# A hand-ordered attention and long-convolution kernel: paired VectorE products and a new order of work

## The chip, the cores and the metric

The kernel runs on one NeuronCore of a Trainium2 chip. It uses five engines, each with its own in-order stream of instructions: TensorE (PE) for matmuls and transposes, VectorE (DVE) and ScalarE (ACT) for elementwise work, GpSimd (POOL) and SyncE (SP), which here mostly issue DMAs. Engines wait for each other by semaphores. The metric is the device time of one execution in microseconds (us); lower is better.

## The reference

Two blocks follow each other. The first is attention with 4 batches, 8 heads, 768 positions and head size 64. A query sees the first 8 keys (global) and the 96 keys up to itself (local); each head has its own slope for a bias that falls with distance. The second is a gated long convolution over the 512 channels.

```
scores = scale * q @ k.T + bias           # bias = -slope[h] * distance
scores = where(is_global | is_local, scores, -1e9)
a = softmax(scores);  x = a @ v           # x: [4, 768, 512]

x1, x2, x3 = split(x @ w_proj, 3)         # 512 columns each
x2_conv = irfft(rfft(x2) * rfft(filter))  # over the 768 positions
out = (x1 * x2_conv * x3) @ w_out
```

All inputs and the output are float32. The kernel computes in float16 with float32 accumulation.

## The kernel before, in words

**Tiling.** Work is done batch by batch, with up to two batches in flight: while `conv(b)` runs, `attention(b + 1)` is mixed into it. Within attention, heads go in four pairs (`hp` 0 to 3) and the keys in seven tiles of 128 (8 global keys and 120 local ones each), which form three groups (`GRP`, group index `gi`, tiles 0-1, 2-3 and 4-6). Of the 768 by 768 scores only a band is computed.

**Attention.** `load_pair` loads q or k of a pair, `turned` transposes it on TensorE and copies it to `QT` or `KT`. For batch 3, `load_tiles` loads q and k by tiles and `cross` transposes them with DMA transposes from SP. `scores` multiplies a pair and group into two PSUM banks, and one ScalarE exponential (line 774) reads both banks and writes 864 elements per partition of the pair's tile `E`. For batch 0 ("near") the bias and mask are added to the scores on TensorE. For batches 1 to 3 the exponential is multiplied by a table of masks on VectorE (line 791). The branch at line 779 can do this for two pairs at once, but `PAIR_M`, the list of the batches and groups that take it, is empty. `values` multiplies `E` by v, `rc` and `xn` divide by the sum, and `transpose_x` turns the result into `xT`.

**Gates and convolution.** `gate` computes x1 and x3 from `xT` and the weights `w`, four matmuls each (line 932). `butterfly` and `conv` do the Fourier transform of x2 as small matmuls and VectorE additions ("proj", line 993; "fwd", lines 676, 690 and 1124; "inv", lines 1023 to 1030). In `spectra` each pair of class spectra X is multiplied on VectorE by two filter tables, `h1` and `h2` (lines 1142 and 1145), into `p1` and `p2`, which are halves of one tile `pp`. Another `conv` step multiplies by the gates and projects with `wo` (line 1059); the result `ot` is stored by SP (line 1070).

**The start.** k0, q0 (pair 0 of batch 0) and k1 come as three 384-KB loads from SP and are cast to float16 ("cast", line 314). The other pairs of batch 0, the filter (768 KB), v, the weights `w` (four loads of 256 KB and one of 512 KB), `wo` and everything of the later batches come from POOL (`load`, line 339), in loads of mostly 96 to 120 KB. The identity used by the transposes is made on POOL between the first loads, and so are the tables of distances. ScalarE makes the sine tables of the transform first, then switches its function table to the exponential. Dummy matmuls ("busy", line 310) stand early in TensorE's stream.

**What sets the order.** `Plan` records about a thousand operations with their dependencies. Nothing schedules them at run time: the string `ORDER` at the top of the file lists every operation by its number, with the engine that does it (P, A, V, G, S) and the PSUM banks it takes, and `schedule` only checks that dependencies precede. `i1b5` puts one dummy matmul on bank 5. So the order of each engine, the choice between ScalarE and VectorE for an evacuation, the sequence of the loads on POOL and that of SP's queue all come from this one text. The waits themselves come from the data.

The functions that the change touches:

Of the kernel before, what the change touches and what calls it, by code (L numbers as in the profile page):

```python
# [17 lines left out]
P = 128  # L18
# [14 lines left out]
def dve(n, rate=1, psum=False):  # L33
    return 0.068 + (0.005 if psum else 0.0) + n / rate / 960.0
# [8 lines left out]
35G 19A 12P2 13A 46V 52G 37A 48V i2b5 83P0 38A 53G 81P3 72G 20V 26A 61G 63G 21A 14V 44V 50V 15V 39V 201P1 93P2  # L43
36V 87P4 84A 202V 57V 60G 43A 82A 207V 95P3 16A 94A 97P67 209V 85P2 65G 64G 29V 11V 62G 88A 41V 91P0 203V 66G
96V 149P45 239G 42A 236G 86V 98A 204A 234G 150A 40V 89P3 121P67 151P45 238G 58V 208V 90V 205V 122A 152A 117P23
92V 99P67 206V 103P45 211V 233G 212V 118A 213V 235G 100A 119P23 101P67 153P01 104A 105P45 120A 102A 154A 27V
214V 115P23 237G 106V 215V 59S 116A 107V 155P67 78A 216V 110P01 111V 128P23 232G 157P45 156A 77A 217V 67G
220P6 112V 162P01 221A 158V 108P6 73A 113P7 129V 130V 123P23 109A 224P6 159V 131P4 114V 79A 222P7 245G 68G
341P5 241G 243G 225A 163V 124V 76A 223A 218P6 31V 240G 164V 125V 337P0 132V 28V 339P1 244G 340V 165P7 126P4
127V 247G 160P2 74A 335P1 338A 137P4 342A 166V 193V 139A 161V 133P7 376P23 219A 242G 336V 246G 354P45 414P01  # L50
377A 138P6 69G 167P2 355A 134P3 415A 183V 135A 184V 351P45 352A 192V 194V 140V 373P01 186V 185V 136V 343P6
374A 459G 169A 248G 195V 172P7 70G 71G 171P4 464G 187V 196V 173A 226P01 347P2 227A 345P3 411P45 251G 344V 252G
353V 349P0 145P6 75A 174V 249S 412A 348V 141P2 346V 254G 357P45 350V 228A 417P01 147A 375V 253G 420P67 188V
168P3 255G 197V 458G 256G 470G 356V 189V 143A 170V 142P2 465G 418A 471G 144V 175P0 358A 146P1 421A 382P67 198V
191V 460G 360P23 177A 413V 199V 148V 80A 190V 383A 379P45 380A 258P0 463G 361A 259A 229P67 416V 200V 378V
271P1 363P45 272A 230A 422V 275P2 461G 364V 273P3 231A 250S 466G 276A 284P6 419V 385P01 362V 274A 384V 286P7
359V 260P2 386V 365V 387V 462G 560P3 287A 479G 478G 285A 469G 261A 368P45 381V 279P0 366P1 472G 561A 473G 369V
468G 277P2 288V 423P67 370V 280A 262P3 289V 264P0 278A 367A 371P1 424V 263A 467G 425V 372A 282V 566P2 428P45
266P1 390P67 257G 265A 706G 567A 562P0 281V 267A 429V 388P3 391V 563A 179P2 430V 564P1 392V 176P4 181A 180P0
565A 389A 269V 576P67 268V 182V 178V 426P1 577A 431P2 393P0 432V 427A 394V 579P45 687G 580A 598P67 639P23 640A  # L60
396P0 698G 572P1 574P4 270V 395P5 298P2 407P3 696G 573A 599A 474G 397A 450V 570P1 568P6 449V 451V 695G 452V
404P5 575A 299A 408P7 694G 409A 403P4 571V 684G 398V 636P23 585P01 453V 410V 690G 569A 283V 454V 405A 600V
637A 582P67 445P4 480G 586A 481G 699S 399P2 447A 406V 433P3 446P4 455V 477G 702G 292P5 583A 435A 401A 456V
457V 645P67 607P01 448V 693G 293A 300P3 638V 646A 290P2 294P5 441P4 295A 304P6 442P5 581V 476S 608A 482G 584V
443A 400P7 475S 578V 302P4 697G 296P0 609V 688G 301A 291A 647V 303A 444V 689G 402V 485P1 604P45 297A 305A 587V
642P23 486A 307V 306V 605A 601P67 641V 691G 643A 685S 483P0 496P1 593P23 602A 308V 594V 603V 497A 484A 498P4
606V 588P67 487P5 589V 683G 701G 499A 595A 437P4 309V 489P0 590V 490A 488A 704G 310V 615P67 439A 692G 644V
311V 703G 610P23 611V 616V 700S 653P01 491P5 617A 438P4 612V 312V 511P2 440V 654V 686S 434P3 313V 596P4 618P6
512A 597A 492A 619A 500P7 655V 591P2 592A 613P5 314V 493V 501A 502P4 509P6 494V 648P01 504P7 656P2 705G 614A
624P5 510A 787S 649V 505A 513V 657A 632P6 503A 436V 315V 620P7 507V 629P4 621P3 626A 323P5 495V 506V 789S 514V  # L70
625P2 650A 508V 785S 634A 622A 651P0 324A 652A 628P6 784S 515P7 786S 517P5 529P1 518A 623V 527P3 627V 316V
675V 523P0 516A 528A 519P2 630A 670P5 525P3 793S 526A 521P7 633P6 530A 520A 791S 332P3 674V 317P2 524A 635V
333A 631V 672A 662P3 522A 803P45 790S 677V 806P67 800P01 318A 664A 801A 788S 676V 326P2 804A 795S 532V 327A
329P3 320P0 678V 330A 321A 796S 707P2 679V 663P3 807A 797P01 531V 680V 794S 825P67 533V 708A 534V 822P45 798A
682V 826A 720P2 666P0 535V 805V 536V 665V 671P3 823A 537V 681V 828P67 673V 721A 819P45 711P1 658P3 668A 820A
712A 799V 792S 829A 724P2 861P01 827V 870P67 660A 867P45 725A 722P3 540V 538V 802V 319S 334S 871A 733P2 868A
539V 723A 709P6 809P45 726P3 541V 734A 808V 554P7 331S 872V 810V 727A 735P3 542P2 830V 811V 862A 863V 555A
710A 814P01 836P45 864P67 736A 815V 543A 824V 837V 667P3 816V 865A 659P2 869V 838A 866V 715P6 713P7 661V
878P01 325S 669V 714A 548P2 728P7 812P3 879V 716A 821V 880V 737V 817P6 831P45 729A 873P01 839P7 322S 832V 730V
818A 813A 874V 551P3 731V 833A 875V 328S 732V 718V 557P6 881P4 738V 834P5 876P0 545P1 840A 835A 882A 877A  # L80
856P7 556S 717V 841P4 904V 741P0 903V 719V 745P5 546A 749P1 558A 742A 843A 549A 746A 857P6 842P0 906V 905V
907V 908V 851P2 858A 909V 750A 753P7 559S 844A 747P5 754A 739P4 743P1 751P0 883P7 744A 912P1 748A 910V 740A
852P4 752A 756V 859A 755V 913A 924P6 853A 936P2 552A 925A 911V 884P5 757V 854A 938P6 914P3 845V 937A 758V
916P2 939A 915A 860V 928P3 759V 888P6 210A 917A 760V 553S 940V 761V 929A 920P4 550S 918P3 886A 919A 926P2 941V
764V 921A 923V 922V 932P3 889P5 927A 898P4 933A 930P3 544S 894P2 885A 946P7 931A 762V 896A 942P3 935V 957P1
846P2 934V 855V 947A 958A 961P7 943A 944P1 962A 948P3 945A 763V 959P0 949A 963P7 960A 964A 765V 951V 950V
847P1 781P0 547S 891A 965V 966V 952V 967V 769P5 899P7 848A 953V 770A 900A 968V 954V 969V 772P2 955V 970V 956V
766P3 849A 773A 971V 850V 974V 774S 901A 972V 893P2 767A 782A 975V 775P7 973V 890A 892V 778P3 771S 895A 897V
982P2 768S 985V 779A 902V 783S 976P3 887V 776A 979P7 986V 983A 987V 993P2 989P6 988V 780S 994P 1001P0 980V
990P 777S 977A 978S 997P7 998P 995A 984S 991A 999A 1002P 1003V 981S 996S 992S 1000S 1004S  # L90
"""


# [105 lines left out]
class Fused:  # L199
# [541 lines left out]
    def scores(self, hp, gi, near=False):  # L741
        nc, g = self.nc, self.g
# [23 lines left out]
        if self.b in self.CROSS:  # L766
# [3 lines left out]
                                    name="near" if near else "scores"))  # L770
# [8 lines left out]
        if (self.b, gi) in self.PAIR_M:  # L779
            if hp % 2:  # L780
                hs = slice(2 * hp - 2, 2 * hp + 2)
                ep = self.EE[:, hp - 1:hp + 1].rearrange("p a h c -> p (a h) c")[
                    :, :, 496 * gi:496 * gi + 496].rearrange("p h (m w) -> p h m w", m=2)[:, :, :, 0:216]
                mk = self.mask[:, hs].rearrange("p h (m w) -> p h m w", m=3)
                mk = (mk[:, :, 0:2], mk[:, :, 1:2].to_broadcast([P, 4, 2, 216]), mk[:, :, 1:3])[gi]
                g.op("V", dve(1728, 2), lambda _: nc.vector.tensor_mul(ep, ep, mk),
                     r=[("mask", h) for h in range(hs.start, hs.stop)], w=[("E", hp - 1, gi), ("E", hp, gi)], name="masked")
            return
        mk = self.mask[:, 2 * hp:2 * hp + 2].rearrange("p h (m w) -> p h m w", m=3)
        mk = (mk[:, :, 0:2], mk[:, :, 1:2].to_broadcast([P, 2, 2, 216]), mk[:, :, 1:3])[gi]  # L790
# [1 line left out]
             r=[("mask", 2 * hp), ("mask", 2 * hp + 1)], w=[("E", hp, gi)], name="masked")  # L792
# [324 lines left out]
    def spectra(self, b, pair):  # L1117
        nc, g, X, DM = self.nc, self.g, self.X, self.DM
# [11 lines left out]
        if n == 2:  # L1130
# [11 lines left out]
        g.op("V", dve(1024, 2), lambda _: nc.vector.tensor_mul(  # L1142
            p1, xs, self.h1[:, n:n + 1].to_broadcast([P, 2, DM])),
             r=rs, w=[("p1", k)], name="prod")
        g.op("V", dve(1024, 2), lambda _: nc.vector.tensor_mul(
            p2, xs, self.h2[:, n:n + 1].to_broadcast([P, 2, DM])),
             r=rs, w=[("p2", k)], name="prod")

        if b in self.SUMPE:
            return  # L1150
# [147 lines left out]
```

## Time and profile before

| What | Value |
| --- | --- |
| median of 3 runs | 164.43 us (164.33 to 164.94) |
| profiled execution | 164.8 us |
| its span, first to last instruction | 163.0 us |
| granted TensorE clock | 0.999 |
| PE busy | 154.0 us (94%) |
| VectorE busy | 151.6 us (93%) |
| ScalarE busy | 150.3 us (92%) |
| POOL busy | 76.8 us (47%) |
| bytes moved by DMA | 21.95 MB |

The profile is of one execution. "Span" runs from the first to the last instruction; the execution's own time is 1.8 us longer. A busy share counts the time in which at least one instruction of the engine was in flight; neighbouring instructions overlap, so the distance between two starts is often shorter than a duration. A row of a timeline or of the chain gives the start in us, the length in us, the engine, the line of the code, and what it writes and reads; "x4" says that four instructions were merged. "[1.85 <-ACT y L498]" says that the engine stood idle for 1.85 us before it, until ScalarE's instruction of line 498 was done.

### The profile page before, as it was taken

The numbers are of one execution on the slowest core, as the hardware profiler recorded it, in microseconds if no ns is written. First come the engines' busy times: TensorE is split into PE (matmuls) and PEld (weight loads), VectorE is DVE, ScalarE is ACT, GpSimd is POOL, SyncE is SP. The second block draws the span as 40 slices with busy tenths as digits, with TensorE's granted clock in tenths as the row PEclk, the third lists the DMA queues.
The fourth block names the chain that finished last, engine by engine and source line by source line (L and its number), as shares of the span: only waits on it lengthen the run. The fifth ranks groups of instructions, "written<-read, shape, count | busy, mean of one in ns | idle before, by whom it ended". The sixth has DMA issues, their size and how long they took to land.

```text
span 163.0 us, 4256 instructions
## 1 busy us (share of the span) xinstructions
PE 154.0 (94%) x1604; PEld 94.7 (58%) x1604; DVE 151.6 (93%) x356; ACT 150.3 (92%) x327; POOL 76.8 (47%) x101
## 2 busy tenths in 40 slices
PE   6599997999999999999999999999999999999980
PEld 2274355866655777666577584445676664584440
DVE  6599699999999999999999999999999999999960
ACT  8999996999999999999999999999998999997850
POOL 7999199999979997999970000000000000000000
PEclk9999999999999999999999999999999999999999
DMA  5999999999999999999999964630100106000684
GB/s 170 200 166 164 165 150 138 147 158 174 190 162 154 139 136 136 149 153 163 161 129 162 134 121 101 236 150 0 64 4 6 66 0 253 5 4 0 264 332 178
DMA packets 84956, 21.95 MB, mean 135 GB/s; under 512 B 75584, under 2 KB 81992, under 8 KB 84936
## 3 DMA queue, kind: packets, MB, share of 16 engines
q0 software_dynamic: 73040, 12.11, 98.4%
q1 hardware_dynamic: 11896, 9.57, 21.4%
q8 instruction: 12, 0.20, 0.5%
q14 instruction: 8, 0.07, 0.1%
HBM read 25.40 MB, written 6.29 MB: 194 GB/s over the span
## 4 chain that ended last, share of the span: by engine, by line
PE 85%; ACT 9%; DVE 3%; issue 1%
PE bank L932 26%; PE bank L993 13%; PE bank L1059 13%; PE bank L759 7%; PE bank L854 4%; PE bank L809 4%; PE bank L707 3%; PE bank L1023 3%; PE bank L1124 3%; PE bank L814 3%; PE bank L753 2%; ACT E L774 2%; ACT KT L314 1%; PE bank L1030 1%; PE bank L690 1%; ACT QT L314 1%
## 5 line engine op out<-in xcount | busy, mean ns | idle before, releaser
L932 PE MATMUL bank<-xT,w 128*128 128x384 f16 x256 | 48.2, 326 | 0.0
L774 ACT ACTIVATE E<-bank 128x864 f16<-128x864 f32 x48 | 41.0, 911 | 0.3 <-PE bank L759 0.2
L932 PEld LDWEIGHTS <-w 128*128 128x128 f16 x256 | 23.9, 98 | 15.8 <-issue 0.3
L339 POOL DMA_DIRECT2D vn<-in_v_dram x28 | 26.3, 979 | 1.1 <-DMA w<-in_moe_w_proj_dram 1.1
L339 POOL DMA_DIRECT2D kn<-in_k_dram x25 | 21.8, 892 | 5.4 <-DMA vn<-in_v_dram 4.0
L1059 PE MATMUL bank<-wo,y 128*128 128x512 f16 (+1 forms) x100 | 22.6, 371 | 0.0
L339 POOL DMA_DIRECT2D qn<-in_q_dram x25 | 21.8, 885 | 0.1
L791 DVE TENSOR_TENSOR E<-E,mask 128x864 f16<-128x864 f16 x36 | 20.3, 591 | 0.0
L318 ACT ACTIVATE x<-bank 128x384 f16<-128x384 f32 x32 | 16.6, 547 | 0.0
L318 ACT ACTIVATE ot<-bank 128x512 f32<-128x512 f32 (+1 forms) x23 | 13.3, 610 | 3.5 <-PE bank L1059 3.1
L809 PE MATMUL bank<-vn,E 128*128 128x65 f16 x224 | 15.3, 193 | 0.9 <-DVE xn L833 0.7
L993 PE MATMUL bank<-w,xs 128*128 128x512 f16 x64 | 15.9, 379 | 0.0
L809 PEld LDWEIGHTS <-E 128*128 128x128 f16 x224 | 14.0, 97 | 2.3 <-DMA vn<-in_v_dram 0.4
L1059 PEld LDWEIGHTS <-y 128*128 128x128 f16 x100 | 9.5, 98 | 9.9 <-DVE y L1113 0.5
L814 PE MATMUL bank<-vn,E 128*128 128x65 f16 x192 | 15.0, 193 | 0.0
L314 ACT CAST eo<-bank 128x384 f16<-128x384 f32 x32 | 14.3, 513 | 0.6 <-PE bank L1030 0.2
L314 ACT CAST X<-bank 128x512 f16<-128x512 f32 x24 | 14.3, 636 | 0.4
L314 ACT CAST ab<-bank 128x512 f16<-128x512 f32 x24 | 14.3, 629 | 0.4 <-PE bank L993 0.3
L833 DVE TENSOR_TENSOR xn<-bank,rc 128x512 f16<-128x512 f32 (+1 forms) x19 | 14.3, 771 | 0.1
L814 PEld LDWEIGHTS <-E 128*128 128x128 f16 x192 | 13.1, 97 | 1.9 <-issue 1.2
L759 PE MATMUL bank<-QT,KT 64*128 64x216 f16 (+2 forms) x224 | 13.7, 242 | 0.0
L759 PEld LDWEIGHTS <-KT 64*128 64x128 f16 x224 | 7.9, 94 | 8.7 <-issue 6.8
(163 smaller groups left out, 334.1 us busy)
## 6 DMA issues: line engine op xcount, KB each, us to landing
out_dram<-ot SPq DMA_DIRECT2D x23, 256.0 KB
vn<-in_v_dram POOLq DMA_DIRECT2D x28, 120.0 KB, 7.6
kn<-in_k_dram POOLq DMA_DIRECT2D x16, 96.0 KB, 5.1
qn<-in_q_dram POOLq DMA_DIRECT2D x16, 96.0 KB, 5.2
w<-in_moe_w_proj_dram POOLq DMA_DIRECT2D x4, 256.0 KB, 5.8
kn<-in_k_dram POOLq DMA_DIRECT2D x7, 120.0 KB, 6.2
g<-in_moe_filter_fft_dram POOLq DMA_DIRECT2D x1, 768.0 KB, 10.6
qn<-in_q_dram POOLq DMA_DIRECT2D x6, 128.0 KB, 7.0
```

The source lines that it names most:

```text
L314: {"A": nc.scalar.copy, "V": nc.vector.tensor_copy, "G": nc.gpsimd.tensor_copy}[e](out, in_)
L318: self.nc.scalar.mul(out, in_, c)
L339: return self.g.op(eng, 0.57 + 0.00035 * nbytes[0] if eng == "G" else 0.5, lambda _: e.dma_start(dst, src), w=w, r=r, nbytes=nbytes, name= ...
L759: nc.tensor.matmul(bs[hh].f32()[:, off:off + w], self.KT[hs, hp, P * m:P * m + P], self.QT[hs, hp, KL * m:KL * m + w], start=(off == 0 and ...
L774: g.op("A", act(864), lambda _: nc.scalar.activation(eo, bs[0].two()[:, :, 0:432].rearrange("p h (m w) -> p h m w", m=2), Act.Exp, scale=s ...
L791: g.op("V", dve(864, 2), lambda _: nc.vector.tensor_mul(eo, eo, mk), r=[("mask", 2 * hp), ("mask", 2 * hp + 1)], w=[("E", hp, gi)], name=" ...
L809: nc.tensor.matmul(o[:, n, hh], ef[:, at:at + P], vt[:, t, 2 * hp + hh, 0:D + 1], start=first, stop=(t == 0), skip_group_check=True)
L814: nc.tensor.matmul(o[:, n, hh], ef[:, at:at + P], vt[:, t - 1, 2 * hp + hh, 0:D + 1], start=False, stop=True, skip_group_check=True)
L833: nc.vector.tensor_mul(to, o[:, :, :, 0:D], rc.to_broadcast([P, 2, 2 * nt, D]))
L932: nc.tensor.matmul(bk.f32()[:, 0:h], self.w[:, c, o + P * j:o + P * j + P], self.xT[:, c, h * s:h * s + h], start=(c == 0), stop=(c == 3))
L993: nc.tensor.matmul(bk.f32(), src[:, c], w[:, c, DM:2 * DM], start=(c == 0), stop=(c == 3))
L1059: nc.tensor.matmul(bk.f32()[:, 0:n], y[:, c, P * t:P * t + P], self.wo[:, c, cs], start=(c == 0), stop=(c == 3))
```

## The change

Three edits are made.

1. `PAIR_M` now lists batches 1 to 3 with all three groups. For these, the mask product is done when the second pair of two has its exponential, as one VectorE instruction of 1728 elements per partition instead of two of 864. There are 18 such instructions instead of 36.
2. `h1` and `h2` become halves of one tile, and the two products of a class pair become one instruction that writes `p1` and `p2`, 2048 elements instead of twice 1024. There are 8 instead of 16. The two products of the last class pair of each batch are left as they are.
3. `ORDER` is replaced. Operations keep their code but change places, some evacuations and small copies change between ScalarE and VectorE, the loads on POOL and the DMAs on SP have another sequence, and there are 8 dummy matmuls instead of 3. The loads themselves are the same.

```
-    PAIR_M = ()
+    PAIR_M = tuple((b, gi) for b in range(1, 4) for gi in range(3))
...
-        self.h1 = t("h1", [P, 4, DM])
-        self.h2 = t("h2", [P, 4, DM])
+        self.hh = t("h", [P, 2, 4, DM])
+        self.h1, self.h2 = self.hh[:, 0], self.hh[:, 1]
...
-        pp = t("pp", [P, 2, 4, DM])
+        self.pp = pp = t("pp", [P, 2, 4, DM])
...
-        g.op("V", dve(1024, 2), lambda _: nc.vector.tensor_mul(
-            p1, xs, self.h1[:, n:n + 1].to_broadcast([P, 2, DM])),
-             r=rs, w=[("p1", k)], name="prod")
-        g.op("V", dve(1024, 2), lambda _: nc.vector.tensor_mul(
-            p2, xs, self.h2[:, n:n + 1].to_broadcast([P, 2, DM])),
-             r=rs, w=[("p2", k)], name="prod")
+        g.op("V", dve(2048, 2), lambda _: nc.vector.tensor_mul(
+            self.pp[:, :, 2 * k:2 * k + 2], xs[:, None].to_broadcast([P, 2, 2, DM]),
+            self.hh[:, :, n:n + 1].to_broadcast([P, 2, 2, DM])),
+             r=rs, w=[("p1", k), ("p2", k)], name="prod2")
```

The start of the order, and of the loads in it (operations by kind, in their sequence on the engine):

```
 ORDER, first line
-0V 1V 2A 3G 45S 30A 47S 4V 34V 6A 9A 32G 56S 49S 5V i1b5 22P0 55G 23A 54G 7G 24A 10V 17P1 8V 33V 25V 51G 18A
+0V 1V 2A 3G 4V 5V 45S 32G i1b6 17P0 10V 12P1 8A 33V 22P2 18A 34V 56S 47S 49S 46V 51G 19A 13A 52G 23A 7G 24V
...
 POOL, batch 0 and 1 (b1 q2 is half of pair 2's q of batch 1)
-q3 k3 identity q1 table k2 q2 filter v1 v3 v0 v5 v4 v2 v6 | b1: k1 q1 k0 k1 q0 k0 q1 q0 w0 q3 w1024 q2 k2 q2 q3 k3 k2 k3 w256 | b2 q0, b1 v0, w1280 w512
+q1 k2 identity q2 q3 k3 table filter v0 v6 v1 v2 v5 v3 | b1: k0 k0, v4, w256 k1 k1 q1 q1 w0 q0 q0 w1024 k3 w1280 q3 q3 k2 k2 q2 k3 q2, v0, w512
...
 VectorE, before the first transpose
-... distances, angles 2 (reads ScalarE's result), cast k0, cast q0, angles 1, ..., cast k1
+... distances, cast k0, cast q0, angles 2, angles 1, ...     (cast k1 is on ScalarE)
...
 SP, transposing DMAs of batch 3 among the stores (q1 is q's tile 1)
-q1 q2 q0 k0 k1 q4 q3 k3 k2 q5 k6 k5 k4, then all stores
+q1 q0 q4 q3 q2 k1 q5 k4 k0 k6 k2 k3, two stores, k5, then the other stores
```

More of the change, by code (lines that the diff above doesn't have):

```diff
@@ L47 @@
[L47 to L56, printed above, removed]
@@ new lines @@
+195V 405P01 73A 343P2 180P3 188V 346V 347P6 196V 408A 406A 167P4 181A 253G 344V 189V 348V 450G 341P2 452G 182V
+461G 254G 409V 369P01 376P67 210V 169A 349P45 142P3 370A 171P0 342V 377A 350A 144V 168P1 373V 410P23 255G
+374P45 356P67 197V 173A 270P0 170V 256G 258P1 411A 198V 375A 191V 412P45 200V 190V 199V 378V 271A 357A 353V
+354P23 413A 175P0 355A 272P6 273A 260P4 359P23 358V 259A 262P6 360V 261A 177A 414V 460G 384P45 263A 284P7
+282P1 285A 266P6 264P0 361V 364P23 463G 550P7 385V 283A 276P1 386V 465G 267A 379P45 265A 277A 172P6 365V 286V
@@ L91 @@
+878V 960V 765S 873V 950P3 957A 759S 953P4 961V 951A 958S 952S 967P5 962V 975P3 968P 963P2 976P 964P 954A 977A
+971P4 972P 965A 955S 969V 970S 973V 978S 966S 974S
 """
@@ L786, in scores @@
                 g.op("V", dve(1728, 2), lambda _: nc.vector.tensor_mul(ep, ep, mk),
-                     r=[("mask", h) for h in range(hs.start, hs.stop)], w=[("E", hp - 1, gi), ("E", hp, gi)], name="masked")
+                     r=[("mask", h) for h in range(hs.start, hs.stop)], w=[("E", hp - 1, gi), ("E", hp, gi)], name="masked2")
             return
```

78 lines of the change are left out of this document (40 added, 38 removed).

## The prediction

> **What bounds the kernel now.** I read the page's shares first, then a table by stretches, then the chain of waits in order of time.
>
> ```profile
> PE 154.0 (94%) x1604; PEld 94.7 (58%) x1604; DVE 151.6 (93%) x356; ACT 150.3 (92%) x327; POOL 76.8 (47%) x101
> PE 85%; ACT 9%; DVE 3%; issue 1%
> ```
> ```profile
> 7.16:28.18 21.02, 19.70 (x261) 11.35 (x262) 19.20 (x53) 19.24 (x35) 16.99 (x22) 1.00 1.77 158
> 28.18:60.00 31.82, 31.82 (x391) 21.58 (x388) 31.55 (x80) 31.34 (x61) 30.57 (x37) 1.00 2.04 158
> 60.00:100.00 40.00, 40.00 (x440) 26.49 (x439) 39.80 (x83) 39.76 (x97) 23.25 (x26) 1.00 1.79 143
> 100.00:151.57 51.57, 51.57 (x473) 30.89 (x472) 51.24 (x106) 48.84 (x109) 0.00 (x0) 1.00 0.18 66
> 151.57:163.00 11.43, 6.94 (x37) 3.24 (x34) 5.81 (x17) 4.89 (x10) 0.00 (x0) 0.99 0.73 275
> ```
> ```profile
> 32.97 1.30 PE bank L932 x8
> ...
> 43.08 2.71 PE bank L932 x16
> ...
> 68.80 2.80 PE bank L932 x16
> ...
> 151.57 6.95 PE bank L1059 x36
> 158.55 0.42 DVE ot L320
> ```
> The columns of the second fence are stretch, length, then busy time of PE, weight loads, DVE, ACT and POOL. From 28.2 to 151.6 us TensorE is never idle, VectorE loses 0.8 us and ScalarE 2.8. The chain runs through PE until 158.5. It has small holes all the same: eight matmuls of a gate take 1.30, so sixteen should take 2.60, and the quoted sixteens took 2.71 and 2.80. From such excesses I estimate about 1 us of waiting in the whole stretch. The amount of matmul work isn't changed, so time can come only from an earlier start of the closed run, from those holes, or from the end.
>
> **The change, part by part.**
>
> Merged products. 18 pairs of mask products and 8 pairs of class products become 26 instructions instead of 52.
>
> ```profile
> 49.59 2.10 DVE L791 TENSOR_TENSOR E<-E,mask 128x864 f16<-128x864 f16 x4
> 59.35 0.68 DVE L1145 TENSOR_TENSOR pp<-X,h 128x1024 f16<-128x1024 f16 x1
> 59.95 0.68 DVE L1142 TENSOR_TENSOR pp<-X,h 128x1024 f16<-128x1024 f16 x1
> ```
> Four mask products in a row take 2.10, the last one 0.59 of it, so they start 0.50 apart; two products of a pair start 0.60 apart. 160 more elements for 0.10 us is 0.6 ns each, so 864 elements are about 0.45 to 0.5 and some 0.07 is left per instruction. 26 x 0.07 = 1.8 us off VectorE. The lower end is 0; the upper one takes the whole lag of duration over the elements, 0.68 - 0.53 = 0.15, times 26 = 3.9. I take 1.8, since VectorE runs back to back and what counts there is the distance of starts. [...] None of the 1.8 is on the path by itself, because TensorE is the closed one; it shortens TensorE's waits on VectorE. Of about 1 us of holes I take 0.2 and keep 0 to 1. The price is that the first mask of a pair is ready only after the pair's second exponential; the order places its readers later, so I take nothing for it.
>
> The start. k0, q0 and k1 come by SP; VectorE casts the first.
>
> ```profile
> 2.00:4.00 2.00, 2.00 (x9) 0.89 (x9) 1.49 (x10) 1.94 (x13) 1.71 (x6) 1.00 0.93 320
> ```
> ```profile
> 5.45 0.29 POOL masks.py:199 TENSOR_SCALAR_AFFINE_SELECT ident<-ident 128x128 f16<-128x128 f16 x1
> ```
> ```profile
> 5.89 0.69 DVE L500 SCALAR_TENSOR_TENSOR y<-y,bank 128x512 f32<-128x512 f32 x1 [1.85 <-ACT y L498]
> 6.50 0.61 DVE L314 CAST kn<-h 128x768 f16<-128x768 f32 x1
> ```
> ```profile
> 7.16 0.82 PE L707 MATMUL bank<-ident,kn 128*128 128x128 f16 x6 [1.86 <-DVE kn L314]
> ```
> ```profile
> 8.54 1.07 ACT L314 COPY KT<-bank 128x720 f16<-128x720 f16 x4
> 12.94 1.28 ACT L774 ACT_TABLE_LOAD   x1
> 14.23 0.89 ACT L774 ACTIVATE E<-bank 128x864 f16<-128x864 f32 x1
> ```
> 640 KB had moved by 4 us (320 GB/s), more than k0's 384 KB, yet its cast stood until 6.50 behind an instruction that waited 1.85 for ScalarE. In the new order both casts stand ahead of that instruction, so the transposes of k0 wait for the identity (5.74) instead: 5.8 for 7.16. ScalarE then takes KT at about 6.7 for 8.54. Between KT and the first exponential it does 5.7 us now; there it gains the third cast and two table steps and loses a KT and a QT, about 6.3 in all, so the first exponential comes near 13.0 for 14.2. Five more dummy matmuls of 512 columns stand behind q0, where TensorE has nothing else; at the 0.82 us that 6 x 128 columns take here, each is 0.55. This same ScalarE work hides them; uncovered they would cost 2.7 us. Six other operations move each way between ScalarE and VectorE and nearly cancel; ScalarE's 2.8 idle us cover the rest.
>
> The loads then take most of it back.
>
> ```profile
> 32.90 1.73 POOL L339 DMA_DIRECT2D kn<-in_k_dram  x2
> 34.52 0.86 POOL L339 DMA_DIRECT2D w<-in_moe_w_proj_dram  x1
> ...
> 36.08 1.05 POOL L339 DMA_DIRECT2D vn<-in_v_dram  x1
> 37.01 1.64 POOL L339 DMA_DIRECT2D w<-in_moe_w_proj_dram  x2
> ```
> ```profile
> DMA packets 13844, 2.88 MB, mean 169 GB/s; under 512 B 11596, under 2 KB 13842, under 8 KB 13842
> ```
> ```profile
> kn<-in_k_dram POOLq DMA_DIRECT2D x1, 96.0 KB, 5.2
> w<-in_moe_w_proj_dram POOLq DMA_DIRECT2D x1, 256.0 KB, 5.7
> vn<-in_v_dram POOLq DMA_DIRECT2D x1, 120.0 KB, 5.6
> w<-in_moe_w_proj_dram POOLq DMA_DIRECT2D x1, 256.0 KB, 6.0
> w<-in_moe_w_proj_dram POOLq DMA_DIRECT2D x1, 512.0 KB, 7.9
> ```
> ```profile
> 40.60 0.51 PE L707 MATMUL bank<-ident,kn 128*128 128x128 f16 x6
> ...
> 46.38 1.04 PE L993 MATMUL bank<-w,xo 128*128 128x512 f16 x4
> ```
> The last numbers are us from issue to landing. The last k load of batch 1 is issued at 33.7 and lands at 38.9; the last weights are issued at 37.8 and land at 45.7, and the product that needs them starts at 46.4. So the old order kept 0.7 to 1.7 us of margin. The loads stream without a pause (the DMA column, second to last, stands at 2.04 there) and their bytes don't change; only the sequence does. In the new sequence the last k load of pair 3 has the same loads ahead of it, less one 96-KB load (96 KB at 169 GB/s, 0.6), plus two quarters of the weights. Their cost: 34.5 + 5.7 = 40.2, 1.3 after the k load; 37.0 + 6.0 = 43.0, 1.3 after the v load at 41.7. It lands at 38.9 - 0.6 + 2.6 = 40.9. Its transposes start at 40.6 now, 117.9 before 158.5. By then the new order has done two more gates (2 x 0.65), one pair of transforms (0.43), and one turn (0.34) and two score groups (0.2 each) fewer: 1.0 us more, so 116.9 is left, and PE's work ends at 40.9 + 116.9 = 157.8 instead of 158.5. Everything the start gains beyond that is lost waiting here. Two filter products and the last v loads stand less close. With 0.3 us for an error in six landings I take 0.6 off.
>
> SP. The last transposing DMA, of k tile 5, now stands behind two stores that wait for ScalarE.
>
> ```profile
> 96.95 3.83 SPq L406 DMA_TRANSPOSE KT<-kn  x3
> 101.01 59.10 SPq L1070 DMA_DIRECT2D out_dram<-ot  x25
> ```
> The stores could first be issued at 101.0; the transpose then runs to about 103 (3.83 / 3 each), and the scores that read it come near 107. It is hidden by 4 us of projections and gates. Each us beyond that would be paid whole.
>
> The end. Now three stores follow each other after the last matmul; in the new order the second half of the last tile is stored before the last piece.
>
> ```profile
> 150.72 9.39 SPq L1070 DMA_DIRECT2D out_dram<-ot  x13
> ```
> Each costs about 0.4 to 0.5 of SP; I take 0.2 off (0 to 0.4).
>
> Sum on the span: 0.6 + 0.2 + 0.2 = 1.0, 163.0 to 162.0. The profiled run took 164.8, 1.8 around its span and 0.4 above the median of the three runs, so I set 1.0 against the median: 164.4 to 163.4.
>
> **The rivals.** (1) No real change: the landing at 40.9 or a margin like the old one holds TensorE and the holes and the end stay: 0.3 off, 164.1. For it: all three engines are full, and only VectorE is relieved. (2) Slower: pulling the weights forward delays the stream at the last q and k of batch 1. POOL already stood 1.1 us for a weight load, and weight loads took 5.2 to 7.9 us to land. From 41.6 on the landing costs more than the old run; at 42.5 the end is 0.9 late, 165.3.
>
> ```profile
> 45.93 0.92 POOL L339 DMA_DIRECT2D vn<-in_v_dram  x1 [1.07 <-DMA w<-in_moe_w_proj_dram]
> ```
> Against it: the total of bytes ahead is fixed. (3) All holes close, since VectorE has 1.8 us to spare: another 0.8, then 162.4 with the end's 0.4. (4) Slower by POOL: if a product of VectorE holds up the issue of a load, a product of twice the length holds it longer.
>
> ```profile
> L339 POOL DMA_DIRECT2D vn<-in_v_dram x28: 908/948/1142, 9.5 to 83.5; - x28
> ```
> The columns are the shortest, median and longest ns of 28 equal issues: the median lies 0.04 over the shortest, the longest 0.23. Some 30 issues between 40 and 60 us would be late by 1.2 more if the median excess doubled, which margins like the 1.7 above still cover, and by 3.5 at half the longest: 1.8 us uncovered, 166.2. [...] (5) The wider products lose their rate, as operands with one more repeated dimension: 18 x 0.9 + 8 x 1.07 = 25 us. Against it: the products now already read repeated operands at the full rate.
>
> **How the numbers follow.** Forecast 0.45, (1) 0.25, (2) 0.15, (3) 0.08, (4) 0.03, (5) 0.02, 0.02 unplaced. A difference under 0.5% (0.8 us, the runs' own spread is 0.6) counts as none, so the line is 163.6: most of the forecast (0.38) and (3) are faster, 0.46; its rest, (1) and the unplaced are the same, 0.34; (2), (4) and (5) slower, 0.20. The range runs from (3) to (2), 162.4 to 165.5; the forecast's own is 162.9 to 163.9.
>
> **What would show it.** Right: k0's cast near 4.2, first exponential near 13, TensorE waiting for kn or w between 30 and 45, mask products of 1728 elements near 1.05 us, last matmul near 158, VectorE with idle time after 60. Wrong: a first exponential after 14, waits of TensorE on masks or on KT of the last batch, products near 2 us.

## The result: 1.0% slower, and the profile after

The changed kernel takes 166.41 us (median of 8 executions, 165.47 to 166.81). The kernel before took 164.50 beside it on the same chip (164.26 to 165.18). The ratio is 1.010 with a 95% interval of 1.0072 to 1.0128. Medians here and below are of all executions, while ratios leave out the few that ran over 1.5% above the fastest of their kernel and are not quotients of the medians. The forecast was 163.4, so even its sign was wrong; the time lies above the range too. The profiled execution took 166.61, its span is 164.8.

The page of the changed kernel, shares and clock:

```profile
PE 155.0 (94%) x1609; PEld 94.4 (57%) x1609; DVE 150.9 (92%) x336; ACT 150.6 (91%) x320; POOL 76.8 (47%) x101
...
PEclk9999969999999999999999999999999999999998
```

VectorE lost 0.7 us of work, yet the run is longer. One new thing stands out: the granted TensorE clock has a slice of 6 tenths, between 20.6 and 24.7 us (each digit stands for a fortieth of the span, 9 for 90% or more). The table by stretches (length, then busy time of PE, weight loads, DVE, ACT and POOL, then the clock, the busy share of the DMA engines and GB/s) says where the time is:

```profile
7.14:34.61 27.47, 24.48 (x320) 13.79 (x321) 22.77 (x69) 25.28 (x48) 24.08 (x32) 0.94 1.78 168
34.61:60.00 25.39, 25.39 (x268) 15.87 (x266) 25.15 (x60) 24.91 (x44) 23.98 (x29) 1.00 2.16 152
60.00:100.00 40.00, 40.00 (x486) 27.25 (x485) 39.72 (x73) 40.00 (x99) 22.65 (x26) 1.00 1.80 130
100.00:157.78 57.78, 57.78 (x510) 34.16 (x508) 57.20 (x113) 53.50 (x118) 0.00 (x0) 1.00 0.26 89
```

From the first gate (34.61) to 157.8 TensorE is never idle; the kernel before was closed like this too. The waits in which TensorE is seen idle lie ahead of that gate, 3.0 us of them behind 7.14; between its first transpose and its closed run the kernel before had 1.3. The timeline has the places to compare:

```profile
34.61 0.81 PE L931 MATMUL bank<-xT,w 128*128 128x384 f16 x4
...
43.84 0.50 PE L706 MATMUL bank<-ident,kn 128*128 128x128 f16 x6
...
155.50 5.35 PE L1058 MATMUL bank<-wo,y 128*128 128x512 f16 x28
```

The first gate starts at 34.61. In the kernel before it started at 32.80:

```profile
32.80 1.46 PE L932 MATMUL bank<-xT,w 128*128 128x384 f16 x8
...
153.80 4.71 PE L1059 MATMUL bank<-wo,y 128*128 128x512 f16 x25
```

The last k turn of batch 1 (the transpose of that k on TensorE), to which the prediction tied the end, is at 43.84 (40.60 before), and TensorE ends at 160.85 (158.51 before). From that turn to the end it is 117.0 us now and was 117.9. So the turn is 3.2 us late, the work behind it 0.9 us shorter, and the rest behind TensorE's end 0.5 us shorter (3.95 in place of 4.49): 1.8 us, the difference of the two spans.

Between 14 and 25 us one chain is seen on three engines of the changed kernel:

```profile
14.49 0.27 ACT L317 ACTIVATE inv<-bank 128x128 f16<-128x128 f16 x1
14.65 0.90 ACT L773 ACTIVATE E<-bank 128x864 f16<-128x864 f32 x1
15.42 0.76 ACT L626 ACTIVATE mask<-eo 128x648 f16<-128x648 bf16 x1
16.05 1.68 ACT L773 ACTIVATE E<-bank 128x864 f16<-128x864 f32 x2
17.60 0.77 ACT L626 ACTIVATE mask<-eo 128x648 f16<-128x648 bf16 x1
18.23 0.31 ACT L317 ACTIVATE inv<-bank 128x128 f16<-128x128 f16 x1
...
20.64 0.89 ACT L773 ACTIVATE E<-bank 128x864 f16<-128x864 f32 x1 [0.81 <-PE bank L758]
```
```profile
18.57 0.23 DVE L319 TENSOR_SCALAR inv<-bank 128x128 f16<-128x128 f16 x1 [1.69 <-ACT inv L317]
18.71 0.95 DVE L313 COPY QT<-bank 128x768 f16<-128x768 f16 x1
```
```profile
19.71 0.52 PE L752 MATMUL bank<-eo 128*128 128x432 bf16 x2 [1.72 <-DVE QT L313]
...
20.54 0.90 PE L752 MATMUL bank<-eo 128*128 128x432 bf16 x2
```

A part of the table `inv` is scaled on VectorE (18.57). It waits 1.69 us for another part of the same tile, which ScalarE scales only at 18.23, behind three exponentials and two mask builds. Behind it on VectorE stands the evacuation of QT, TensorE's near scores wait for that, and ScalarE's exponentials wait for the scores. The matmuls behind TensorE's wait are slow as well: 0.90 for two bias matmuls, where the same two take 0.54 before the wait.

### The profile page after: what moved, and what is told of

It reads as the page before. It is cut to its first block, busy times and chain, and to the rows that moved or that the text cites. A ratio compares the mean times of both kernels' runs of the same rounds, so it can differ in the third digit from the quotient of the medians.

```text
span 164.8 us, 4248 instructions
## 1 busy us (share of the span) xinstructions
PE 155.0 (94%) x1609; PEld 94.4 (57%) x1609; DVE 150.9 (92%) x336; ACT 150.6 (91%) x320; POOL 76.8 (47%) x101
## 4 chain that ended last, share of the span: by engine, by line
PE 85%; ACT 7%; DMA 3%; DVE 1%; issue 1%; SPq 1%; DVEq 0%
PE bank L931 26%; PE bank L992 13%; PE bank L1058 13%; PE bank L758 6%; PE bank L808 4%; PE bank L853 4%; PE bank L706 4%; ACT E L773 4%; PE bank L1022 3%; PE bank L813 3%; PE bank L1123 3%; DMA h<-in_q_dram 3%; PE bank L752 2%; PE bank L309 1%; PE bank L1029 1%; PE bank L689 1%
## 5 line engine op out<-in xcount | busy, mean ns | idle before, releaser
L931 PE MATMUL bank<-xT,w 128*128 128x384 f16 x256 | 48.7, 326 | 0.0
L773 ACT ACTIVATE E<-bank 128x864 f16<-128x864 f32 x48 | 41.6, 945 | 2.0 <-PE bank L758 1.6
L785 DVE TENSOR_TENSOR E<-E,mask 128x1728 f16<-128x1728 f16 x18 | 18.4, 1041 | 0.0
L317 ACT ACTIVATE x<-bank 128x384 f16<-128x384 f32 x32 | 17.4, 576 | 0.3 <-PE bank L931 0.2
L317 ACT ACTIVATE ot<-bank 128x512 f32<-128x512 f32 (+1 forms) x23 | 13.9, 622 | 3.9 <-PE bank L1058 3.7
L808 PE MATMUL bank<-vn,E 128*128 128x65 f16 x224 | 15.6, 193 | 0.7 <-ACT E L773 0.7
L313 ACT CAST ab<-bank 128x512 f16<-128x512 f32 x24 | 15.2, 655 | 0.5 <-PE bank L992 0.4
L813 PE MATMUL bank<-vn,E 128*128 128x65 f16 x192 | 15.3, 193 | 0.0
L758 PE MATMUL bank<-QT,KT 64*128 64x216 f16 (+2 forms) x224 | 14.2, 247 | 0.0
```

The lines of the kernel that those rows point to most:

```text
L313: {"A": nc.scalar.copy, "V": nc.vector.tensor_copy, "G": nc.gpsimd.tensor_copy}[e](out, in_)
L317: self.nc.scalar.mul(out, in_, c)
L758: nc.tensor.matmul(bs[hh].f32()[:, off:off + w], self.KT[hs, hp, P * m:P * m + P], self.QT[hs, hp, KL * m:KL * m + w], start=(off == 0 and ...
L773: g.op("A", act(864), lambda _: nc.scalar.activation(eo, bs[0].two()[:, :, 0:432].rearrange("p h (m w) -> p h m w", m=2), Act.Exp, scale=s ...
L808: nc.tensor.matmul(o[:, n, hh], ef[:, at:at + P], vt[:, t, 2 * hp + hh, 0:D + 1], start=first, stop=(t == 0), skip_group_check=True)
L813: nc.tensor.matmul(o[:, n, hh], ef[:, at:at + P], vt[:, t - 1, 2 * hp + hh, 0:D + 1], start=False, stop=True, skip_group_check=True)
```

## The experiments

Theory F: the loss lies wholly ahead of the first gate, in the order of work. Its main rival, M: the merged products cost the time, because a mask comes later than it did. The measured times, each against the kernel before on the same chip:

| Run | Median us | Ratio to before (95%) |
| --- | --- | --- |
| before (over all these runs) | 164.5 to 164.8 | 1 |
| the changed kernel | 166.41 | 1.010 (1.0072 to 1.0128) |
| e1 old order, merged products | 166.83 | 1.011 (1.0063 to 1.0154) |
| e2 new order, split products | 167.54 | 1.015 (1.0097 to 1.0198) |
| e8 old order, only class products merged | 164.58 | 0.997 (0.9937 to 1.0011) |
| e4 new order, one scaling early | 164.62 | 0.999 (0.9969 to 1.0019) |
| e9 new order, wait filled with dummies | 165.44 | 1.006 (1.0024 to 1.0087) |
| e3 new order, one dummy for six | 166.83 | 1.011 (1.0053 to 1.0157) |
| e5 e4 and the folded table late | 164.89 | 1.000 (0.9966 to 1.0039) |
| e6 e5 and one dummy for six | 164.73 | 1.000 (0.9966 to 1.0026) |
| e7 e5, two dummies, start reordered | 164.53 | 0.998 (0.9941 to 1.0020) |
| e10 all mended, folded table on ScalarE | 164.43 | 1.001 (0.9982 to 1.0027) |
| e11 all mended, folded table on VectorE | 163.39 | 0.994 (0.9913 to 0.9960) |
| e12 as e11, products split | 164.56 | 0.999 (0.9974 to 1.0009) |

### Which part of the change costs the time

e1 takes the products alone, e2 the order alone.

```
 e1: the old ORDER, with the new product code
-... masked(hp 0) ... masked(hp 1) ...     prod p1, prod p2
+... ............ ... masked2(hp 0, 1) ... prod2
```

> The order of work of the kernel before, with the merged products of the kernel after: each merged mask product stands where the second of its pair stood, each merged complex product where its first stood; nothing else is moved. Theory F (the 1.9 us were lost ahead of the first gate, by the new order, and the merged products lie under TensorE): the first gate starts at 32.8 as before, VectorE's busy time falls by about 2 us, and the time is 163.8 to 164.6 (before 164.5). Theory M (the merged products cost the time, because the mask of the first pair of a head group comes later than it did and the product of values waits for it): 165.5 to 167, with TensorE waiting for the tile E behind the mask line in the batches 1 to 3.

```
 e2: the new ORDER, with the old product code
-masked2(hp 0, 1)                prod2
+masked(hp 0) masked(hp 1)       prod p1, prod p2
```

> The order of the kernel after, with every merged product split into its two parts again, side by side at its place: 26 instructions more on VectorE. Theory F: the first gate starts at 34.6 as in the kernel after, and the time is 166.4 (the split products hidden) to 168.2 (all 26 x 0.07 us on the path). Theory M: 164.2 to 165.0, the loss gone with the merged products.

Each part alone makes the kernel slower, by 1.1 and 1.5%. Theory F's figure for e1, 163.8 to 164.6, was wrong, and so was M's for e2, 164.2 to 165.0. Each was right where it expected a loss. In e1 the first gate is not late (32.27), and the loss lies behind it: TensorE ends 120.1 us behind the last k turn of batch 1, 117.9 in the kernel before. TensorE's waits in e1, and VectorE's timeline at one of them:

```profile
PE bank L807 <- DVE xn L831: 1.3, 3, 0.7
...
PE bank L807 <- DVE E L784: 0.4, 1, 0.4
```
```profile
79.32 1.98 DVE L784 TENSOR_TENSOR E<-E,mask 128x1728 f16<-128x1728 f16 x2
...
81.62 0.68 DVE L831 TENSOR_TENSOR xn<-bank,rc 128x512 f16<-128x512 f32 x1
```
```profile
82.36 0.19 PE L807 MATMUL bank<-vn,E 128*128 128x65 f16 x1 [0.36 <-DVE xn L831]
```

The columns of the first fence are us in total, times, and the longest. Two merged masks stand in a row here, where the old order had one, two and one single masks with other work between (the last one behind `xn`), and `xn` behind them frees its PSUM bank late. In the kernel before that `xn` stood at:

```profile
81.17 0.68 DVE L833 TENSOR_TENSOR xn<-bank,rc 128x512 f16<-128x512 f32 x1
```

TensorE's values product waits 0.36 us for that bank; one wait is on the mask itself (0.4). The kernel before has one wait for `xn`, of 0.7, and none for a mask. e8 undoes the mask part.

```
 e8: the old ORDER, prod2 for each pair of products; PAIR_M = ()
```

> The order of the kernel before with only the complex products merged (8 instructions less on VectorE); the masks stay apart. Theory V (in the order of before it is the mask of the first pair, moved back to the second's place, that values products wait for: 0.52, 0.60, 0.56 and 0.37 us on TensorE in the run with all products merged): those four waits are gone and the time is 164.2 to 164.9, as before or up to 0.5 us less. Rival P (the wider complex products hold up others on VectorE): 165.5 to 166.8.

164.58, not to be told from the kernel before, and TensorE waits once for `xn` again, 0.6, and for no mask. So in the old order it is the merged masks that cost, as theory V had it. The new order gains from the merge instead. The intervals of e2 and the changed kernel overlap, so the 0.5% between them proves little, but their profiled executions agree up to the last k turn of batch 1 (43.77 and 43.84), and behind it TensorE needs 118.3 us with the products split and 117.0 with them merged.

### The wait at 18.57

e4 moves one instruction of 0.3 us.

```
 ScalarE
-... inv(1) exp mask exp exp mask inv(2) copy exp ...
+... inv(1) inv(2) exp mask exp exp mask copy exp ...
```

> The kernel after with one instruction moved on ScalarE: the second scaling of the inverse table (0.3 us), which VectorE's third scaling of that table waits for, stands right behind the first one, ahead of three exps and two mask builds. Theory F2 (VectorE's wait of 1.69 us at 18.57 holds up the evacuation of q tile 2, the near scores at 19.7, and then three exps by 0.81, 0.42 and 0.42): that wait is under 0.3 us, the near scores start at 18.0 to 18.3, the last near exp ends at 27.5 to 28.2 in place of 29.2, the first gate starts at 33.0 to 33.8 and the time is 164.8 to 165.6. Rival: the loads (vn, the first weights) or ScalarE's own sum of work hold the first gate, and the time is 166.2 to 166.6 with the wait gone.

164.62: 1.8 us less than the changed kernel. Theory F2's direction was right and its size too small: 164.62 lies 0.2 us under its range, and the first gate 0.6 ahead of its earliest place. VectorE, ScalarE and TensorE of e4:

```profile
16.94 0.21 DVE L318 TENSOR_SCALAR inv<-bank 128x128 f16<-128x128 f16 x1
```
```profile
18.94 4.06 ACT L772 ACTIVATE E<-bank 128x864 f16<-128x864 f32 x5
```
```profile
32.43 0.81 PE L930 MATMUL bank<-xT,w 128*128 128x384 f16 x4
...
41.66 0.50 PE L705 MATMUL bank<-ident,kn 128*128 128x128 f16 x6
```

The wait is gone, five exponentials follow each other without a gap, and the first gate is 2.2 us earlier. The loads or ScalarE's work did not hold it; that rival falls.

A part of the 1.8 us may be the clock rather than the wait. The table by stretches of the changed kernel around it (columns as above; the clock is the figure behind POOL's):

```profile
18.00:19.71 1.71, 0.00 (x1) 0.01 (x1) 1.14 (x3) 1.71 (x4) 0.96 (x2) 1.00 2.46 149
...
21.00:22.00 1.00, 1.00 (x7) 0.27 (x6) 0.93 (x4) 0.58 (x2) 1.00 (x2) 0.50 2.42 154
...
24.00:24.50 0.50, 0.50 (x6) 0.11 (x2) 0.50 (x1) 0.36 (x2) 0.50 (x1) 1.00 1.72 187
```

After 1.7 us without a matmul the granted clock is 0.50 at 21 to 22 us, and 1.00 again at 24. e9 leaves the wait as it is and keeps TensorE busy in it.

```
 TensorE
-... near(18.0 ends)          near(19.71) ...
+... near(18.0 ends) busy x6  near(19.71) ...
```

> The kernel after with nothing moved, and six dummy matmuls on TensorE ahead of the near scores at 19.71, in the time in which they wait for VectorE (18.0 to 19.3). They shorten no wait. Theory G (a part of the loss is TensorE's granted clock, 0.58 and 0.57 of full speed from 20 to 24 us behind a stretch with 0.29 us of work in 2 us): the granted clock stays 1.0, the three near scores behind take 0.82 in place of 1.31, 1.31 and 1.03, ScalarE's two gaps of 0.42 us close, and the time is 165.3 to 165.8. Rival (the wait alone counts; the slower matmuls were covered by the exps): 166.2 to 166.6. Theory F2 says in both cases that most of the 1.9 us stays.

165.44, about 1.0 us less than the changed kernel. The table by stretches of e9 and a row of its timeline:

```profile
18.00:20.00 2.00, 1.82 (x12) 0.70 (x8) 1.36 (x3) 1.90 (x4) 1.08 (x2) 1.00 2.42 150
20.00:22.00 2.00, 2.00 (x18) 0.57 (x16) 1.93 (x8) 1.36 (x2) 2.00 (x3) 1.00 2.40 150
```
```profile
20.53 0.54 PE L751 MATMUL bank<-eo 128*128 128x432 bf16 x2
```

The clock stays at 1.00, the two bias matmuls take 0.54 instead of 0.90, and the first gate starts 1.3 us earlier. So of the 1.8 us that e4 regained, about half was the slow clock that the wait brought on, and the rest the wait: 1.0 and 0.8 by the medians, 0.7 and 1.0 by the ratios. The intervals of e9 and the changed kernel overlap, so the split is rough; that the clock stays up is plain.

e3 asks about the dummies behind q0.

```
-... turn(q0) busy x6 turn(q1) ...
+... turn(q0) busy x1 turn(q1) ...
```

> The kernel after with one dummy matmul in place of the six that stand on TensorE ahead of the turn of q tile 1. Theory F1 (the dummies hold back the first turns by 2 us, and with them the first exp): q tile 1 is turned at 8.4 in place of 10.3, the first exp starts at 12.4 to 12.8 in place of 13.7, ScalarE comes to the evacuation that VectorE waits for 0.9 to 1.3 us sooner, and the time is 165.1 to 165.6. Theory W (the work behind is held by VectorE and ScalarE, and the dummies only fill TensorE's wait): 166.2 to 166.6. Theory K (the dummies keep TensorE's clock up): without them the turns and near scores up to 17 us take longer, 166.6 to 167.5.

The turn of q1 comes at 8.55 in place of 10.30 and the first exponential at 13.65, so W was right about the first exponential: ScalarE's queue sets it. The median, 166.83, is no gain and lies in K's range. But the six executions lie far apart: 165.32 and 165.42 with a mean granted clock of 0.996 and 0.995, the other four 166.64 to 167.27 with 0.974 to 0.990. The profiled one (165.42) has the wait on VectorE, 1.56 us, TensorE idle for 1.59 us behind it, and no slow clock after that (1.00 from 20 to 24 us). In the profiled execution of e2 (167.79) TensorE is idle for 1.6 us at the same place, and the clock row has an 8 and a 6 in the two slices from 16.6 to 24.9 us. The clock rows of the two, e2 first:

```profile
PEclk9999869999999999999999999999999999999999
```
```profile
PEclk9999999999999999999999999999999999999998
```

So of two waits of about the same length one was followed by the slow clock and the other not. For the executions without a profile only the mean clock is on record, not where it fell. They fit: all executions of e4 and e9, which have no such idle time, have 0.994 or more, and of the eight of the changed kernel four took 166.6 to 166.8 with 0.986 to 0.988 and two 165.5 and 165.9 with 0.995 and 0.994 (of the other two one, 166.11 with 1.0, doesn't fit). Whether K's cause, a slow start without the dummies, adds to the four long executions of e3 stays open.

### Mending the rest of the front

e5 moves the folded table out of the row of exponentials.

```
 ScalarE, on top of e4
-... exp foldp exp exp xT kT xT mask mask h ...
+... exp exp exp xT kT xT foldp mask mask h ...
```

> As the run with the early scaling of the inverse table, and on ScalarE the folded table (foldp, 1.26 us, read by TensorE only after the first gates) stands behind the evacuation of the second transposed x, not ahead of the last two near exps. Theory F (the first gate is held by the chain of near exps on ScalarE): the last near exp ends at 25.8 in place of 27.0, TensorE's wait of 0.74 us ahead of the values product at 27.08 goes, the first gate starts 0.5 to 1.0 us sooner than 32.43, and the time is 163.6 to 164.2. Rival (x's evacuations and the forward products, then the masks on ScalarE, hold the first gate): 164.4 to 164.9, with the wait standing one step further on.

164.89, no gain. The wait it was to remove is gone, and stands one step further on in e5, as the rival said:

```profile
31.06 0.38 PE L852 MATMUL bank<-ident,xn 128*128 128x128 f16 x4 [0.93 <-ACT h L316]
```

e6 takes five of the six dummies out again, now without the wait.

```
-... turn(q0) busy x6 turn(q1) ...
+... turn(q0) busy x1 turn(q1) ...
```

> The run with the late folded table, with one dummy matmul for the six ahead of q tile 1. Theory W (ScalarE's queue, 9.2 to 27 us without a pause, sets the first exp, and the six dummies only fill a wait of TensorE): within 0.4 us of the run with the late folded table. Theory F1 (the dummies hold back the turns): 0.4 to 1.2 us less. Theory K (they keep the clock up): 0.5 to 2 us more in some executions, with a granted clock of 0.97 to 0.99 and near scores of 1.3 us in place of 0.82, as the kernel after with one dummy showed.

164.73, within 0.2 us of e5, as W had it: the dummies were hidden. (The 1.3 us that K takes from e3 are 1.19 in e3's profile, from 10.87 to 12.06.) e7 changes the start.

```
 on top of e5; TensorE: two dummies for six
 POOL    -q1 k2 identity ...             +identity q1 k2 ...
 VectorE -... slope vfirst near ... angles1  +... slope x4 angles1 near vfirst ...
 ScalarE three slopes less; sines(0) ahead of qT(1)
```

> The run with the late folded table, two dummies for six, and a start in another order: GpSimd makes the identity ahead of two load issues, VectorE takes three slope scalings from ScalarE, and the reduction of the first angles goes ahead on VectorE, so that ScalarE's third sine is not behind it. Theory F (what comes off the front comes off the end): identity at 4.3 in place of 5.9, k tile 0 turned at 4.8 to 5.0 in place of 5.95, first exp at 12.5 to 13.0 in place of 13.75, and the time 0.6 to 1.2 us under the run with the late folded table. Rival L (the loads, issued 0.75 us later, or VectorE's queue, full from 9 us on, take it back): within 0.3 us of that run.

The first exponential comes at 12.47, but the time is 164.53, 0.4 us under e5, between what F and L expected, and inside the spread of e7 (163.33 to 165.65). In the profiled execution (165.27) TensorE ran its first near scores slowly, and ScalarE stood behind a scaling on VectorE whose input TensorE makes after those scores:

```profile
11.05 0.90 PE L751 MATMUL bank<-eo 128*128 128x432 bf16 x2
```
```profile
15.21 0.45 ACT L316 ACTIVATE inv<-bank 128x128 f16<-128x128 f16 x2 [1.85 <-DVE inr L318]
```

e10 puts these together: e7's start, with seven dummies around q0's turn, an exponential ahead of the scaling, an evacuation of KT ahead of another, two h ahead of a mask build each, and the folded table behind the x of the first gates. (The h are evacuations of the filter tables; the expectation calls them hidden states.)

```
 on top of e4, e7's start
 TensorE -turn(k0)         turn(q0) busy x6 turn(q1)  +turn(k0) busy x3 turn(q0) busy x4 turn(q1)
 ScalarE -exp inv(1) inv(2) exp      +exp exp inv(1) inv(2)
 ScalarE -exp foldp exp exp ... x1 x1       +exp exp exp ... x1 x1 foldp
 VectorE -inr kT(2)                  +kT(2) inr
 ScalarE -mask mask h mask h h       +mask h h mask h mask
```

> A version with the waits found so far taken out of the order of the kernel after: the second scaling of the inverse table early on ScalarE, the identity ahead of two load issues on GpSimd, three slope scalings on VectorE, the first angles' reduction early, three dummy matmuls on each side of q tile 0's turn (7 with the four behind it) so that TensorE does not stand idle from 5.4 us on, the second exp ahead of the table scalings, k tile 2's evacuation ahead of one of them, the folded table behind the first gates' factors, and two hidden states' evacuations ahead of a mask build each. Theory F: first exp 11.9 to 12.5, near scores at 0.82 us from the first, last near exp 25.0 to 25.6, the first gate at 30.6 to 31.4, from there 126.3 us to the end of TensorE, and the time 162.6 to 163.6, 0.7 to 1.3 per cent under before. Rival L (the loads): the first weights (30.3) or the last k tile (39 to 40) hold the gates, and the time is 164.0 to 164.6.

The first gate starts at 30.91, as F had it, and the time is 164.43, as L had it, but no load is what TensorE waits for. The folded table now stands ahead of two exponentials on ScalarE, and TensorE's scores wait for these:

```profile
37.31 1.35 ACT L316 ACTIVATE fold<-fold,part 128x128 f16<-128x128 f16 x4
38.48 1.74 ACT L772 ACTIVATE E<-bank 128x864 f16<-128x864 f32 x2
```
```profile
40.28 0.56 PE L757 MATMUL bank<-QT,KT 64*128 64x216 f16 x12 [0.99 <-ACT E L772]
```

e11 makes that table on VectorE, in an idle time of it; e12 is e11 with all products split.

```
 e11, on top of e10: foldp from ScalarE (behind x1) to VectorE (behind the first butterflies)
 e12, on top of e11
-masked2(hp 0, 1)                prod2
+masked(hp 0) masked(hp 1)       prod p1, prod p2
```

> The version with the waits taken out, and the folded table made on VectorE, in the 0.65 us for which VectorE stood idle at 36.5, instead of on ScalarE at 37.3, where its 1.36 us kept two exps back and TensorE's scores behind them (a wait of 0.99 at 39.3). Theory F: the first gate stays at 30.7 to 31.1, the wait at 39.3 goes, TensorE is without a wait from 34 us on and ends 126.3 us behind the first gate, at 157.0 to 157.6; the time is 162.8 to 163.5. Rival L (the loads): the turns of k tiles 2 and 3 of batch 1, which land at 38.2 and 39.5, or q tile 2 at 40.1, now wait; TensorE's end stays at 158.0 to 158.7 and the time is 163.9 to 164.5.

> The version of the run beside it, with all merged products split into their parts again at the same places (26 instructions more on VectorE). Theory V (with the front mended, the merged products are worth what they showed between the kernel after and its split form, 1.1 us of median and 1.3 us behind the first gate): 1.0 to 1.5 us above the run beside it, with TensorE's waits behind masks and gates in the batches 1 to 3. Rival (hidden under TensorE): within 0.3 us of it.

e11 takes 163.39 us, 0.6% less than the kernel before, with an interval that leaves out 1, and 1.6% less than the changed one by the two ratios. The first gate is at 30.78 and the turn at 40.57:

```profile
40.57 0.50 PE L705 MATMUL bank<-ident,kn 128*128 128x128 f16 x6
```

TensorE ends at 157.63, again 117.06 behind that turn. In the changed kernel, e4, e10 and e11 the turn lies at 43.84, 41.66, 41.76 and 40.57, and TensorE ends 117.0, 117.0, 117.0 and 117.1 later. So what the front gained up to this turn reached the end of TensorE whole. e12 has its turn at the same place, 40.54, and takes 164.56, 1.2 us more, with TensorE's end 118.4 behind the turn. VectorE's masks in e11 and in e12:

```profile
48.01 2.99 DVE L784 TENSOR_TENSOR E<-E,mask 128x1728 f16<-128x1728 f16 x3
```
```profile
48.21 3.19 DVE L790 TENSOR_TENSOR E<-E,mask 128x864 f16<-128x864 f16 x6
```

Three merged masks take 0.20 less than six single ones, about 0.07 for each instruction saved. The chains of the two kernels, e11 first:

```profile
PE 81%; ACT 7%; DVE 5%; DMA 2%; issue 1%; SPq 1%; DVEq 0%; ACTq 0%
```
```profile
PE 58%; DVE 19%; DMA 9%; ACT 5%; SPq 4%; issue 2%; DVEq 0%
```

With the split products the chain runs through VectorE for 19%, though the list of TensorE's waits names none behind a mask. The merged products' own worth in an order that leaves them room is 1.2 us.

## Why the prediction was wrong, step by step

**What bounds the kernel** was read rightly: in the changed kernel TensorE is closed again from the first gate on, and the time is set by when the closed run starts.

**Merged products.** The price came out: 1041 ns for a merged mask, 1213 for a merged class product, no loss of rate, and about 0.07 us saved for each mask. There was luck in it. The step's 0.6 ns an element makes 0.52 us of 864 elements, more than the 0.50 between two starts, so its rows leave nothing over (its 0.45 of 864 elements and 0.53 of 1024 are estimates that no row shows); and VectorE's whole busy time differs by 1.1 us (before and e1), 1.4 (e2 and the changed kernel) and 0.9 (e12 and e11), not by 1.8. The worth was mis-sized. The step took 0.2 us of it for the time and allowed 1; e11 against e12 has 1.2, and in the new order TensorE's work behind the last k turn is 1.3 shorter with them than in e2. "The order places its readers later, so I take nothing for it" holds in the new order; in the old one the late masks cost about 2 us (e1 against e8).

**The start** was right up to ScalarE's KT. The changed kernel's rows:

```profile
4.09 0.69 DVE L313 CAST kn<-h 128x768 f16<-128x768 f32 x1
...
5.96 0.80 PE L706 MATMUL bank<-ident,kn 128*128 128x128 f16 x6 [1.32 <-POOL ident masks.py:199]
...
6.79 1.09 ACT L313 COPY KT<-bank 128x720 f16<-128x720 f16 x4
...
10.87 0.80 ACT L313 COPY QT<-bank 128x768 f16<-128x768 f16 x1 [0.33 <-PE bank L709]
...
13.71 0.89 ACT L773 ACTIVATE E<-bank 128x864 f16<-128x864 f32 x1
```

4.09, 5.96 and 6.79 stand against 4.2, 5.8 and 6.7. The first exponential came at 13.71, not 13.0: from KT it took 6.9 us, not 6.3, a third of a us of that an idle time behind q1's turn. The five extra dummies were hidden, as said (e5 and e6, and in e3 the first exponential comes only 0.06 earlier without them). ScalarE's idle time between 28.2 and 151.6 was misread, 3.45 us by the rows and not 2.8; nothing hangs on it.

**The step that failed is "The loads then take most of it back".** It has the last k load of batch 1 land at 40.9 and hold its turn. The load was issued at 33.79 and took 5.3 us:

```profile
kn<-in_k_dram POOLq DMA_DIRECT2D x1, 96.0 KB, 5.3
```

It landed at 39.1, 1.8 us sooner than the working had it, and its turn came 4.7 us later still. "TensorE waiting for kn or w between 30 and 45" did not happen. The two quarters of the weights ahead of this load were to cost it 2.6 us, less 0.6 for one load fewer; it landed 0.2 later than in the kernel before. POOL had begun with batch 1 earlier, which the working left out. It issued the first of these loads at 14.89 and the second at 18.48, where the old order issued its first at 19.93 (before, then changed):

```profile
19.93 0.86 POOL L339 DMA_DIRECT2D kn<-in_k_dram  x1 [4.03 <-DMA vn<-in_v_dram]
```
```profile
18.48 0.84 POOL L338 DMA_DIRECT2D kn<-in_k_dram  x1 [2.72 <-DMA g<-in_moe_filter_fft_dram]
```

How much of the 1.8 us that explains, no run shows. What came last was the order itself. The working follows the start as far as the first exponential, and then goes straight to the landings; it has no term for the 20 us between. There the wait of `inv` on VectorE, the near scores and the exponentials behind it, and the slow clock put the first gate 1.8 us behind that of the kernel before. The step had PE's work end at 157.8; it ended at 160.85, 3.05 us later. In e4, with one instruction moved, it ends at 158.64: 2.2 of the 3.05 us (1.8 of the median) are the term that was missing. Most of the other 0.85 lies ahead of the turn too (41.66 in e4, 40.9 in the working), about what the first exponential was late; no run takes that part alone. Which part of `inv` is on which engine, and behind what, stands in the order, so the wait could have been read there; the slow clock could not. The other half of the step was right: 116.9 us were to be left from that turn, and 117.0 were.

**SP.** No wait for KT of the last batch appears in the changed kernel; right, though the stores were issued at 103.8 and the last transpose ended at 106.1, 3 us behind the working. **The end.** 0.5 us came off, where the step had 0.2 and allowed 0.4.

**The rivals.** Rival 2, slower, had the sign and the wrong mechanism: the last q and k of batch 1 landed at 39.8 and 39.1 (40.9 and 38.9 before), far from its 41.6, and nothing waited for them. Rival 1 had a landing hold TensorE, which none did. POOL's issues were no longer than before (28 loads of v take 939 ns each, 979 before), so rival 4 falls (that a product holds up an issue at all, no run shows), and the merged products keep their rate, so rival 5 falls. Rival 3, all holes close, is nearest to what the products were found to be worth.

## What to carry to other kernels

Where one engine is closed for most of the run, follow a new order engine by engine through the whole stretch ahead of the closed run, and not only to its first landmark: an instruction of 0.3 us on one engine, placed behind five others, held up three engines here and cost 1.8 us, the slow clock behind it included. Merging two instructions paid here only in an order that has room for the later result; try the merge and the order apart, since each alone cost over 1% and together, with one instruction moved, they cost nothing. A wait of the matmul engine cost its clock here (0.50 behind 1.7 us without a matmul) beside its length, so look at the granted clock behind each.

## What the runs showed of the hardware that was not expected

In the changed kernel the granted TensorE clock fell to 0.50 after 1.7 us without a matmul, and stayed under 1 until about 24 us. That cost 0.7 to 1.0 us (e9), about as much as the wait. In e2 about 1.6 us without a matmul were followed by the slow clock in the profiled execution (an 8 and a 6 in its row), in e3 1.59 us were not (1.00 from 20 to 24 us); what makes the difference, no run shows.

In e7 and e3 the first near scores ran slowly, 0.90 us for two bias matmuls, at about 11 us, in stretches whose granted clock the profile gives as 1.00. In e7:

```profile
10.00:12.00 2.00, 2.00 (x20) 0.93 (x19) 1.91 (x8) 1.98 (x3) 2.00 (x3) 1.00 1.17 165
```

So these slow matmuls early in a run are seen in their durations and not in the clock's row. With seven dummies around q0's turn (e11) the first near scores take 0.54.
